# Weight conversion with its clamp moved to GpSimd and its shifted word in PSUM, and three weight tiles placed first

## The chip, the cores and the metric

The kernel runs on one core of one Trainium2 chip. The metric is the device time of one execution in microseconds. Three executions of the kernel before took 1049.48, 1051.94 and 1058.58 us (median 1051.94).

## The reference, cut to what matters

Top-32 attention over 4 batches, 8 heads, 576 tokens and head dimension 64 feeds two dense blocks. Attention keeps, in each row of scores, the 32 largest, and the output is a softmax over those. The first dense block mixes each token with the one before it and computes `sigmoid(xr @ w_r) * (relu(xk @ w_k)^2 @ w_v)`; the second one is `h = gelu(x @ w_in)`, split into u and v, v normalised, mixed over tokens by `w_sg`, multiplied by u, `x + (...) @ w_out`. The weights `w_r, w_k, w_v, w_in, w_out` arrive as float64; the kernel sees them as pairs of 32-bit words and has to turn them into float32 itself, once, before the dense blocks use them.

## The kernel before, in words

**Attention.** Work is cut into 80 row tiles called slots (128 query rows; mostly two heads in one slot). For a slot, `emit_S` (L230) multiplies on TensorE and ScalarE copies the scores to SBUF (L240); `emit_topk` (L255) finds the 32nd largest score on VectorE: an elementwise max and min of the two halves of a row (L272, L273), rounds of MAX8 (L281, L292) and MATCH_REPLACE8 (L287), and at last the masked product with the row sum (L308), after an exponential on ScalarE (L307). `emit_T` (L311) transposes the result through PSUM, and `emit_unit` (L337) multiplies with v and divides by the sums (L372). The q and k rows of a pair of heads are prepared by `prep_pieces` (L158): a copy and a subtraction split each value into two parts (ScalarE L98 or L172, GpSimd L100 or L173), TensorE transposes them, ScalarE copies them out.

**Weight conversion.** `conv` (L380) handles one tile of 128 x 512 weights: 32 tiles of float64 weights, and 5 of `w_sg` that take another branch. For a float64 tile the order is:

- SyncE issues the load of 512 KB of words (L416); H is the high word of each pair, L the low one
- ScalarE takes the absolute value of H, read as a float (L421)
- VectorE clamps it (L422), shifts it by three bits (L423) and joins it with the sign and exponent bits of H (L424)
- ScalarE scales the low word (L425), GpSimd adds it (L426)
- `split` (L96) makes the two parts of the result (ScalarE L98, GpSimd L100), and SyncE stores them to DRAM (L429), from where `wload` (L440) fetches them for every use.

Raw words and intermediate take two of 12 buffers called ring, the result one of 6 called w. The dense blocks (`part1` L478, `part2` L670) take the mixed rows (L489 to L497, the first product is at L502) and the stored weights. Their last adds are at L727, a normalisation at L633.

**Order.** Nothing is ordered by hand but through priorities: `at(p)` (L70) gives what is emitted in it priority p, smaller first. With them a planner (L888) sets, at compile time and by its own model of durations, the order in which each engine's queue holds its instructions. Queues run in that order. Start-up (L774 to L786) has the smallest number and holds the loads and preparation of the first pair of heads, the loads of the second, small constants and the first two slots' scores. Slot s gets 1000*s (L791); up to four conversions are emitted per slot with 1000*(s-4) (L809), dense items with 1000*(s+5)+500 (L816). PSUM has three pools of banks: one for scores, three banks of tag `tp` for transposes and attention output, three of tag `d` for dense products.

Of the kernel before, what the change touches and what calls it, by code (L numbers as in the profile page):

```python
# [11 lines left out]
I32 = mybir.dt.int32  # L12
U32 = mybir.dt.uint32
AF = mybir.ActivationFunctionType
OP = mybir.AluOpType
# [4 lines left out]
CLO = 2.0 ** -15  # L20
CHI = 122879.9921875


def computation(ctx, tc, dram, wscr, flag, fast, q, k, v, mu_k, mu_r, w_k, w_v, w_r, w_in, g_ln, w_sg, b_sg, w_out, out):
    nc = tc.nc
    B, H, S, D = q.shape
# [55 lines left out]
    def bank(tag, shape=(128, 512), dt=F32):  # L82
        if tag == "d" and rows[0] == NROWS:
            tag = ("d", "tp")[turn[0] % 2]
            turn[0] += 1
        return psum.tile(list(shape), dt, tag=tag, name=tag, bufs=BUFS[tag])
# [4 lines left out]
    def ring(shape, name, dt=F32R):  # L91
        return sb.tile(shape, dt, tag="ring", name=name, bufs=NRING)
# [3 lines left out]
    def split(hi, lo, src):  # L96

        nc.scalar.activation(hi, src, AF.Copy)  # L98
        e = nc.vector if tail[0] else nc.gpsimd
        e.tensor_tensor(lo, src, hi.bitcast(F32), op=OP.subtract)  # L100
# [57 lines left out]
    def prep_pieces(su):  # L158

        su.kst, su.qst = {}, {}
        pieces = []
        has1 = 1 in su.chs
        j0, j1 = 2 * su.chs[0], 2 * su.chs[-1] + 2
        nj = j1 - j0
        st = {}

        def spl3(sp, src):  # L170
            n = src.shape[1]
            nc.scalar.activation(sp[:, :n, 0::2, :], src[:, :, None, :].to_broadcast([128, n, 2, D]), AF.Copy)  # L172
            nc.gpsimd.tensor_tensor(sp[:, :n, 1, :], src, sp[:, :n, 0, :].bitcast(F32), op=OP.subtract)  # L173

        def spl_q(h):
            sp = sb.tile([128, 4, 3, D], F32R, tag="splq", name="splq", bufs=1)
            st["q", h] = sp
            spl3(sp, su.raw["q"][:, 4 * h + j0:4 * h + j1, :])

        def spl_k(h):  # L180
            sp = sb.tile([128, 4, 2, D], F32R, tag="splk", name="splk", bufs=1)
            st["k", h] = sp
            split(sp[:, :, 0, :], sp[:, :, 1, :], su.raw["k"][:, 4 * h:4 * h + 4, :])

        def spl_rem():
            sp = sb.tile([128, 2, 3, D], F32R, tag="splr", name="splr", bufs=1)
            st["r"] = sp
            if has1:
                spl3(sp[:, 0:1], su.raw["q"][:, 8:9, :])
            split(sp[:, 1, 0, :], sp[:, 1, 1, :], su.raw["k"][:, 8, :])  # L190

        def main_q(h, c):
            su.qst[h, c] = sb.tile([128, 2, 256], F32R, tag="qst", name="qst", bufs=4)
            ps = bank("tp", (128, 2, 2, 128), F32R)
            j = 2 * (c - su.chs[0])
            for a in range(2):
                for i in range(2):
                    nc.tensor.transpose(ps[:, a, i, :], st["q", h][:, j + i, a:a + 2].rearrange("p a d -> p (a d)"),
                                        identr)
            nc.scalar.activation(su.qst[h, c], ps.rearrange("p a i m -> p a (i m)"), AF.Copy)  # L200

        def main_k(h):
            su.kst[h] = sb.tile([128, S], F32R, tag="kst", name="kst", bufs=4)
            ps = bank("tp", (128, 4, 128), F32R)
            for j in range(4):
                nc.tensor.transpose(ps[:, j, :], st["k", h][:, j].rearrange("p a d -> p (a d)"), identr)
            nc.scalar.activation(su.kst[h][:, 64 * h:64 * h + 512], ps.rearrange("p j m -> p (j m)"), AF.Copy)

        def rem():
            ps = bank("tp", (128, 4, 128), F32R)  # L210
            nc.tensor.transpose(ps[:, 0, :], st["r"][:, 1, 0:2].rearrange("p a d -> p (a d)"), identr)
            for h in range(2):
                nc.scalar.activation(su.kst[h][:, 512 - 512 * h:576 - 512 * h], ps[:, 0, 64 * h:64 * h + 64], AF.Copy)
            if has1:
                for a in range(2):
                    nc.tensor.transpose(ps[:, 1 + a, :], st["r"][:, 0, a:a + 2].rearrange("p a d -> p (a d)"), identr)
                su.qrem = qrems[su.p % 2]
                nc.scalar.activation(su.qrem[:, :, 0::2, :], ps[:, 1:3, :].rearrange("p a (h m) -> p a h m", h=2),
                                     AF.Copy)

        pieces.append(spl_rem)
        for h in range(2):
            pieces.append(lambda h=h: (spl_k(h), main_k(h)))
            pieces.append(lambda h=h: (spl_q(h), main_q(h, su.chs[0])))
            if len(su.chs) == 2:
                pieces.append(lambda h=h: main_q(h, 1))
        pieces.append(rem)
        return pieces
# [151 lines left out]
    def conv(key):  # L380

        kind, i = key
        w = sb.tile([128, 2, 512], F32R, tag="w", name="w", bufs=NW)
        if kind == "sg":
            n = 128 if i < 4 else 64
            raw = ring([128, 5, 128], "rawsg", F32)
            nc.sync.dma_start(raw[:, :4, :n], w_sg[:512, 128 * i:128 * i + n].rearrange("(j p) s -> p j s", p=128))
            nc.sync.dma_start(raw[:64, 4, :n], w_sg[512:, 128 * i:128 * i + n])
            nat = ring([128, S], "nat", F32)
            ps = bank("d", (128, 4, 128))  # L390
            for j in range(4):
                nc.tensor.transpose(ps[:n, j, :], raw[:, j, :n], ident)
            nc.scalar.activation(nat[:n, :512], ps[:n].rearrange("p j m -> p (j m)"), AF.Copy)
            ps = bank("d")
            nc.tensor.transpose(ps[:n, :64], raw[:64, 4, :n], ident[:64, :64])
            nc.scalar.activation(nat[:n, 512:], ps[:n, :64], AF.Copy)
            for hf in range(2):
                if hf:
                    w = sb.tile([128, 2, 512], F32R, tag="w", name="w", bufs=NW)
                split(w[:n, 0, :HALF], w[:n, 1, :HALF], nat[:n, HALF * hf:HALF * hf + HALF])  # L400
                scr = dram.tile([128, 2, HALF], F32, name=f"ws_sg{i}_{hf}")
                nc.sync.dma_start(scr[:n], w[:n, :, :HALF].bitcast(F32))
                wscr["sg", i, hf] = scr
            return
        raw = ring([128, 512, 2], "raw64", I32)
        if kind in ("r", "k", "u"):
            src = {"r": w_r, "k": w_k, "u": w_in}[kind]
            s = src[:, 256 * i:256 * i + 256].rearrange("(c p) f -> p c f", p=128)
        elif kind == "v":
            m, half = divmod(i, 2)  # L410
            s = w_v[512 * half:512 * half + 512, 256 * m:256 * m + 256].rearrange("(c p) f -> p c f", p=128)
        elif kind == "h":
            s = w_in[128 * i:128 * i + 128, 1024:].rearrange("p (c f) -> p c f", f=256)
        else:
            s = w_out[128 * i:128 * i + 128, :].rearrange("p (c f) -> p c f", f=256)
        nc.sync.dma_start(raw.rearrange("p (c f) t -> p c (f t)", c=4), s)  # L416
        H, L = raw[:, :, 1], raw[:, :, 0]
        t2 = ring([128, 2, 512], "cvt", F32)
        a, bb = t2[:, 0], t2[:, 1]
        ai, bi = a.bitcast(I32), bb.bitcast(I32)  # L420
        nc.scalar.activation(a, H.bitcast(F32), AF.Abs)  # L421
        nc.vector.tensor_scalar(a, a, CLO, CHI, op0=OP.max, op1=OP.min)  # L422
        nc.vector.tensor_scalar(ai, ai, 3, 0x3FFFFFFF, op0=OP.logical_shift_left, op1=OP.bitwise_and)  # L423
        nc.vector.scalar_tensor_tensor(bi, H, -0x40000000, ai, op0=OP.bitwise_and, op1=OP.bitwise_or)  # L424
        nc.scalar.activation(ai, L.bitcast(U32), AF.Copy, scale=2.0 ** -29)  # L425
        nc.gpsimd.tensor_tensor(bi, bi, ai, op=OP.add)  # L426
        split(w[:, 0], w[:, 1], bb)
        scr = dram.tile([128, 2, 512], F32, name=f"ws_{kind}{i}")
        nc.sync.dma_start(scr, w.bitcast(F32))  # L429
        wscr[key] = scr  # L430

    convq = deque()
# [332 lines left out]
    for i, t in enumerate(slots):  # L765
        if t.last and t.su.p == NP - 1:
# [3 lines left out]
            elif t.u.ch == 1:  # L770
# [4 lines left out]
    start.__enter__()  # L775
    load_raw(supers[0], [("k", 0, 0), ("q", 0, 0), ("k", 0, 1), ("k", 1, 1), ("k", 1, 0), ("q", 1, 0), ("q", 0, 1),
                         ("q", 1, 1)])
    for pc in prep_pieces(supers[0]):
        pc()
    load_raw(supers[1], "kq")  # L780
# [7 lines left out]
    for s, t in enumerate(slots):  # L788
# [20 lines left out]
        with at(1000 * (s - 4)):  # L809
            for _ in range(min(4, len(convq))):  # L810
                conv(convq.popleft())
# [81 lines left out]
```

## Time and profile before

| what | value |
|---|---|
| runs | 1049.48, 1051.94, 1058.58 us |
| profiled execution | 1051.33 us, of which the span from first to last instruction is 1049.6 us |
| TensorE (PE) busy | 902.5 us, 86% |
| VectorE (DVE) busy | 905.5 us, 86% |
| ScalarE (ACT) busy | 714.9 us, 68% |
| GpSimd (POOL) busy | 490.9 us, 47% |
| granted TensorE clock, mean | 0.906 |

The shares are means over stages that differ. Busy time by stretch, the chain of waits and the groups of one stretch say which engine a stage waits for; a group's mean duration, set beside the shortest instruction in it, says whether its instructions were held up while they ran.

### The profile page before, as it was taken

What the parts mean: (1) busy time and instruction counts of PE and PEld (TensorE: products, weight loads), DVE (VectorE), ACT (ScalarE), POOL (GpSimd) and SP (SyncE); (2) the same over time, 40 slices, a digit from 0 to 9 for tenths busy, and PEclk for the clock granted to TensorE, in tenths of its full rate; (3) what the DMA queues carried; (4) which work ended last, traced back from release to release, by engine and by line L of the source; (5) the groups of instructions that cost most, each with busy time, mean ns of one, the idle gap of its engine ahead of it and who ended that gap; (6) DMA issues with size and microseconds to landing.
All of it is one profiled execution on the core that took longest, in us unless ns stands there. A gap on an engine that the chain in (4) does not pass through costs nothing.

```text
span 1049.6 us, 18933 instructions
## 1 busy us (share of the span) xinstructions
PE 902.5 (86%) x6158; PEld 770.7 (73%) x6158; DVE 905.5 (86%) x2541; ACT 714.9 (68%) x1589; POOL 490.9 (47%) x592
## 2 busy tenths in 40 slices
PE   5144645579989998987899999999999998999997
PEld 4132544468879887855789888878899987799895
DVE  5999999999899999999999999899999989712142
ACT  7666876767898786655778669866786597554340
POOL 3676968823493235660934213679242117310051
PEclk8556656879999998976999999999999999999999
DMA  6676865657755543430334443246333423865432
GB/s 181 202 239 226 253 221 190 203 195 257 262 179 180 181 157 110 146 129 1 95 97 125 121 144 100 67 164 198 110 112 115 133 87 103 300 239 153 115 108 65
DMA packets 103405, 164.36 MB, mean 157 GB/s; under 512 B 19200, under 2 KB 72960, under 8 KB 103296
## 3 DMA queue, kind: packets, MB, share of 16 engines
q1 hardware_dynamic: 103296, 163.05, 48.4%
q8 instruction: 51, 0.84, 0.3%
q14 instruction: 58, 0.48, 0.1%
HBM read 133.09 MB, written 29.92 MB: 155 GB/s over the span
## 4 chain that ended last, share of the span: by engine, by line
PE 40%; DVE 40%; ACT 7%; issue 6%; POOL 4%; DMA 2%; SPq 1%; POOLq 0%; DVEq 0%; ACTq 0%
DVE M L281 9%; DVE T L287 9%; PE d L502 7%; PE d L567 7%; DVE E L308 7%; PE d L691 4%; DVE T L272 3%; PE d L612 3%; PE tp L502 2%; DVE T L273 2%; DVE M L292 2%; PE S L238 2%; PE tp L361 2%; PE tp L321 2%; PE d L719 2%
## 5 line engine op out<-in xcount | busy, mean ns | idle before, releaser
L281 DVE MAX8 M<-T 128x8 f32<-128x288 f32 x576 | 237.7, 444 | 1.7
L287 DVE MATCH_REPLACE8 T<-M,T 128x288 f32<-128x288 f32 x432 | 187.8, 439 | 0.0
L502 PE MATMUL d<-xm,w 128*128 128x288 f32 (+2 forms) x1008 | 159.4, 307 | 5.4 <-ACT xm L98 2.7
L502 PEld LDWEIGHTS d<-xm,w 128*128 128x128 f32 x1008 | 142.9, 195 | 8.7 <-ACT xm L98 3.1
L238 PE MATMUL S<-kst,qst 128*128 128x288 f32 x512 | 115.7, 345 | 36.4 <-ACT S L240 20.6
L308 DVE SCALAR_TENSOR_TENSOR E<-S,kth,E 128x576 f32<-128x576 f32 x144 | 139.4, 1000 | 1.4 <-ACT E L307 0.6
L321 PE MATMUL tp<-ident,E 128*128 128x128 f32 x512 | 85.0, 303 | 53.9 <-DVE E L308 29.8
L238 PEld LDWEIGHTS S<-kst,qst 128*128 128x128 f32 x512 | 85.6, 214 | 46.3 <-ACT S L240 25.2
L321 PEld LDWEIGHTS tp<-ident,E 128*128 128x128 f32 x512 | 66.6, 155 | 59.9 <-ACT cvt L425 23.4
L307 ACT ACTIVATE E<-S,nb 128x576 f32<-128x576 f32 x144 | 105.0, 770 | 1.2
L567 PE MATMUL d<-ksq,w 128*128 128x288 f32 (+2 forms) x672 | 101.9, 300 | 0.0
L240 ACT ACTIVATE S<-S 128x576 f32<-128x576 f32 x128 | 83.6, 653 | 19.3 <-PE S L238 18.2
L567 PEld LDWEIGHTS d<-ksq,w 128*128 128x128 f32 x672 | 91.8, 188 | 0.2
L322 ACT ACTIVATE PT<-tp 128x512 f32<-128x512 f32 x128 | 74.3, 599 | 18.8 <-PE tp L321 18.2
L272 DVE TENSOR_TENSOR T<-S 128x576 f32<-128x576 f32 (+1 forms) x81 | 70.5, 870 | 10.8 <-ACT S L240 10.8
L361 PE MATMUL tp<-PT,rawv 128*64 128x256 f32 (+1 forms) x512 | 77.3, 449 | 0.7 <-ACT PT L322 0.7
L691 PE MATMUL d<-w,vn 128*128 128x288 f32 (+1 forms) x420 | 72.5, 313 | 3.0 <-POOL vn L100 1.1
L100 POOL TENSOR_TENSOR splk<-rawk,splk 128x256 fp32r<-128x256 f32 x40 | 32.4, 811 | 86.0 <-ACT splk L98 73.0
L273 DVE TENSOR_TENSOR T<-S 128x576 f32<-128x576 f32 (+1 forms) x80 | 71.5, 893 | 0.0
L691 PEld LDWEIGHTS d<-w,vn 128*128 128x128 f32 (+1 forms) x420 | 59.2, 190 | 12.6 <-issue 6.7
L100 POOL TENSOR_TENSOR ksq<-tmp,ksq 128x576 fp32r<-128x576 f32 (+2 forms) x32 | 38.2, 1196 | 54.9 <-ACT ksq L98 54.8
L426 POOL TENSOR_TENSOR cvt<-cvt 128x512 int32<-128x512 int32 x32 | 46.8, 1464 | 31.8 <-ACT cvt L425 30.2
(162 smaller groups left out, 2045.6 us busy)
## 6 DMA issues: line engine op xcount, KB each, us to landing
w<-ws_k SPq DMA_DIRECT2D x40, 512.0 KB, 4.1
w<-ws_v SPq DMA_DIRECT2D x40, 512.0 KB, 4.1
w<-ws_r SPq DMA_DIRECT2D x20, 512.0 KB, 6.0
w<-ws_h SPq DMA_DIRECT2D x20, 512.0 KB, 4.0
w<-ws_u SPq DMA_DIRECT2D x20, 512.0 KB, 3.7
w<-ws_sg SPq DMA_DIRECT2D x32, 288.0 KB, 3.2
w<-ws_o SPq DMA_DIRECT2D x16, 512.0 KB, 5.0
rawk<-in_k_dram SPq DMA_DIRECT2D x40, 128.0 KB, 2.3
```

Source lines behind the costliest of these rows:

```text
L238: nc.tensor.matmul(ps[:, hf, :HALF], lhsT=su.qst[h, t.u.ch][:, a, 128 * t.i:128 * t.i + 128], rhs=su.kst[h][:, HALF * hf:HALF * hf + HALF] ...
L272: nc.vector.tensor_tensor(T[:, h, :HALF], t.S[:, h, :HALF], t.S[:, h, HALF:], op=OP.max)
L273: nc.vector.tensor_tensor(T[:, :, HALF:], t.S[:, :, :HALF], t.S[:, :, HALF:], op=OP.min)
L281: nc.vector.max(M[:, h, 8 * r:8 * r + 8], src[h])
L287: nc.vector.match_replace(L[h], M[:, h, 8 * r:8 * r + 8], src[h], NEG)
L307: nc.scalar.activation(E, Sx, AF.Exp, bias=nb[:, h:h + 1], scale=0.125)
L308: nc.vector.scalar_tensor_tensor(E, Sx, kv[h], E, op0=OP.is_ge, op1=OP.mult, accum_out=u.sums[:, c + h:c + h + 1])
L321: nc.tensor.transpose(ps[:, kc, :], E[:, h, 64 * h + 128 * kc:64 * h + 128 * kc + 128], ident)
L361: nc.tensor.matmul(px[64 * h:64 * h + 64, :n], lhsT=vr[:, 4 * h + kc, :], rhs=u.PT[h][:, kc, :n], start=(kc == 0), stop=False)
L502: nc.tensor.matmul(ps[:, :n_], lhsT=w[:, bb, 128 * c:128 * c + 128], rhs=act[ch, which, c][:, a, o:o + n_], start=(c == 0 and i == 0), sto ...
L567: nc.tensor.matmul(ps[:, :nn], lhsT=w[:, bb, 128 * (f % 4):128 * (f % 4) + 128], rhs=kt[f][:, a, o:o + nn], start=(f == 0 and i == 0), sto ...
L691: nc.tensor.matmul(ps[:, :HALF], lhsT=act[b, "vn", i][:nn, a, 128 * m:128 * m + 128], rhs=W["sg", i, si][:nn, bb, :HALF], start=(j == 0), ...
```

## The change

In `conv`, the clamp goes from VectorE to GpSimd (its two operations in the opposite order); the shifted word is written into a new bank of tag `tp` instead of SBUF, and the join reads it there. In start-up, up to three conversions (here three tiles of `w_r`) are emitted between the loads and the preparation of the first pair of heads.

```diff
         nc.scalar.activation(a, H.bitcast(F32), AF.Abs)
-        nc.vector.tensor_scalar(a, a, CLO, CHI, op0=OP.max, op1=OP.min)
-        nc.vector.tensor_scalar(ai, ai, 3, 0x3FFFFFFF, op0=OP.logical_shift_left, op1=OP.bitwise_and)
-        nc.vector.scalar_tensor_tensor(bi, H, -0x40000000, ai, op0=OP.bitwise_and, op1=OP.bitwise_or)
+        nc.gpsimd.tensor_scalar(a, a, CHI, CLO, op0=OP.min, op1=OP.max)
+        pi = bank("tp").bitcast(I32)
+        nc.vector.tensor_scalar(pi, ai, 3, 0x3FFFFFFF, op0=OP.logical_shift_left, op1=OP.bitwise_and)
+        nc.vector.scalar_tensor_tensor(bi, H, -0x40000000, pi, op0=OP.bitwise_and, op1=OP.bitwise_or)
         nc.scalar.activation(ai, L.bitcast(U32), AF.Copy, scale=2.0 ** -29)
...
                          ("q", 1, 1)])
+    for _ in range(min(3, len(convq))):
+        conv(convq.popleft())
     for pc in prep_pieces(supers[0]):
```

## Rows read from the trace of the kernel before

**Rows 1.** Busy time by stretch: us, then each engine's busy us, clock, DMA share, GB/s.
```profile
0.00:26.20 26.20, 13.86 (x62) 11.14 (x62) 14.26 (x43) 18.43 (x41) 10.14 (x25) 0.88 0.65 181
26.20:236.20 210.00, 110.72 (x635) 85.98 (x636) 209.04 (x501) 144.33 (x324) 148.97 (x139) 0.66 0.65 216
236.20:892.20 656.00, 626.94 (x4489) 539.18 (x4489) 628.97 (x1898) 489.38 (x1093) 302.41 (x382) 0.97 0.43 135
892.20:1049.60 157.40, 150.94 (x976) 134.43 (x974) 53.21 (x102) 62.79 (x133) 29.36 (x47) 0.99 0.50 163
472.30:498.60 26.30, 20.70 (x110) 15.26 (x109) 26.03 (x86) 15.54 (x35) 1.53 (x4) 0.68 0.00 1
```

**Rows 2.** The chain of work that ended last, share of the span by engine.
```profile
PE 40%; DVE 40%; ACT 7%; issue 6%; POOL 4%; DMA 2%; SPq 1%; POOLq 0%; DVEq 0%; ACTq 0%
```

**Rows 3.** Groups by line and shape, whole span: count | busy us, mean ns | idle before.
```profile
L100 POOL TENSOR_TENSOR w<-cvt,w 128x512 fp32r<-128x512 f32 x32 | 49.5, 1557 | 4.6 <-ACT w L98 4.6
L426 POOL TENSOR_TENSOR cvt<-cvt 128x512 int32<-128x512 int32 x32 | 46.8, 1464 | 31.8 <-ACT cvt L425 30.2 <-DMA rawv<-in_v_dram 1.3
L424 DVE SCALAR_TENSOR_TENSOR cvt<-raw,cvt 128x512 int32<-128x512 int32 x32 | 32.9, 1028 | 0.0
L422 DVE TENSOR_SCALAR cvt<-cvt 128x512 f32<-128x512 f32 x32 | 24.1, 752 | 1.3 <-ACT cvt L421 1.2
L423 DVE TENSOR_SCALAR cvt<-cvt 128x512 int32<-128x512 int32 x32 | 22.2, 693 | 0.0
```

**Rows 4.** Lines 423, 727 and 633: shortest/median/longest ns, first and last start.
```profile
L423 DVE TENSOR_SCALAR cvt<-cvt x32: 402/498/1500, 21.2 to 226.4; 128x512 int32<-128x512 int32 x32
...
L727 DVE TENSOR_TENSOR xr<-d,xr x12: 668/684/692, 705.9 to 1040.3; 128x512 f32<-128x512 f32 x10, 64x512 f32<-64x512 f32 x2
...
L633 POOL TENSOR_SCALAR tmp<-vraw,bag x20: 763/772/1912, 283.5 to 1009.7; 128x512 f32<-128x512 f32 x16, 64x512 f32<-64x512 f32 x4
```

**Rows 5.** Groups of VectorE, 26.2 to 236.2 us.
```profile
L308 DVE SCALAR_TENSOR_TENSOR E<-S,kth,E 128x576 f32<-128x576 f32 x28 | 27.2, 1005 | 0.2
...
L273 DVE TENSOR_TENSOR T<-S 128x576 f32<-128x576 f32 x12 | 13.6, 1132 | 0.0
...
L372 DVE TENSOR_TENSOR x<-tp,rb 128x256 f32<-128x256 f32 x5 | 2.0, 408 | 0.0
```

**Rows 6.** Groups of VectorE, 472.6 to 498.6 us.
```profile
L308 DVE SCALAR_TENSOR_TENSOR E<-S,kth,E 128x576 f32<-128x576 f32 x7 | 5.4, 802 | 0.0
...
L273 DVE TENSOR_TENSOR T<-S 128x576 f32<-128x576 f32 x2 | 1.5, 750 | 0.0
...
L372 DVE TENSOR_TENSOR x<-tp,rb 128x256 f32<-128x256 f32 x1 | 0.4, 407 | 0.0
```

**Rows 7.** Waits, 26.2 to 236.2 us: us in total, times, longest.
```profile
POOL cvt L426 <- ACT cvt L425: 29.8, 16, 4.1
PE tp L321 <- DVE E L308: 26.5, 8, 7.9
ACT cvt L425 <- DVE cvt L424: 26.1, 19, 3.4
...
ACT w L98 <- POOL cvt L426: 3.6, 7, 1.0
```

**Rows 8.** Start of the timeline: start us, us, engine, line, tile.
```profile
6.79 0.33 SPq L156 DMA_DIRECT2D rawk<-in_k_dram  x1
...
10.70 0.46 DVE L272 TENSOR_TENSOR T<-S 128x288 f32<-128x288 f32 x1 [8.71 <-ACT S L240]
```

**Rows 9.** The chain in order of time, 10 to 30 us: start us, us.
```profile
14.19 5.54 DMA raw<-in_moe_w_r_dram
```

**Rows 10.** Timeline: first row of the third slot; first dense product.
```profile
41.80 1.71 DVE L272 TENSOR_TENSOR T<-S 128x576 f32<-128x576 f32 x1
...
176.61 0.76 PE L502 MATMUL d<-xm,w 128*128 128x256 f32 x2
```

**Rows 11.** Waits of SyncE's queue, whole span.
```profile
SPq L429 <- POOL w L100: 90.0, 29, 13.0
```

## The prediction

> **What bounds the kernel now.** I read the table of busy time by stretch first, because the 86% of VectorE and the 86% of TensorE are means over stages with different limits [rows 1]. From 26.2 to 236.2 us VectorE is busy 209.0 of 210 us, while TensorE is busy 110.7 and GpSimd 149.0: in this stage VectorE sets the pace. All but one or two of the 32 conversions of float64 tiles run in it. From 236.2 to 892.2 us VectorE (629 of 656) and TensorE (627) are both near full, and the last 157 us belong to TensorE alone (151). The chain of waits agrees: 40% on each of the two [rows 2].
>
> Then the groups by line and shape, to see what the conversions take from VectorE: lines 422, 423 and 424 cost 24.1 + 22.2 + 32.9 = 79.2 us [rows 3]. Line 423 needs 402 ns at its shortest, but 693 on the mean, and up to 1500 [rows 3, 4]: most of these instructions are held up while they run. The same holds for the top-32 work with two SBUF inputs: line 308 takes 1005 ns here and 802 in a stretch in which GpSimd is busy 1.5 of 26.3 us; line 273 takes 1132 and 750 [rows 1, 5, 6]. Line 372, which reads one operand from PSUM, takes 408 and 407: it is not stretched [rows 5, 6]. So GpSimd's work costs VectorE time in instructions with SBUF operands alone, and not, as far as a row shows, where an operand lies in PSUM.
>
> **The change, part by part.**
>
> *Clamp off VectorE.* 32 instructions of line 422 go: 24.1 us [rows 3].
>
> *Join reads PSUM.* The nearest row is line 727, 512 elements with one operand in PSUM: 684 ns, never over 692 [rows 4]. I take it: 32 x 0.684 = 21.9 against 32.9 us, 11.0 us less. Bounds: as short as 0.668 (0.5 us better), or unchanged at 1.028, then nothing.
>
> *Shift writes PSUM.* No row shows VectorE writing PSUM. It may keep the shortest time of line 423, 402 ns (9.3 us less than now), or cost what the join costs now, 1028 (10.7 us more). I take the PSUM row of the same length, 684 ns: 22.2 - 21.9 = 0.3 us less. The Trainium skill speaks against this edit (VectorE: DVE Perf Modes, Why PSUM operands drop a tier): an operand in PSUM takes fp32 off the double rate. The trace agrees in so far as no PSUM row of this length is below 668 ns. Priced by line 423's shortest time, the edit would lose 32 x (0.684 - 0.402) = 9.0 us, and the whole sum below would be 13 instead of 22. I go by the 693 that it costs in this stage.
>
> These three make 24.1 + 11.0 + 0.3 = 35.4 us less for VectorE in a stage in which it has no other slack.
>
> *Clamp on GpSimd.* The nearest row is line 633, a two-step scalar instruction on 512 elements: 772 ns median, 763 at least [rows 4]; no row has min or max there. The upper bound is the dearest conversion step there, 1557 [rows 3]: 24.4 to 49.8 us more GpSimd work, and I take 24.7. With it GpSimd is busy 149.0 + 24.7 = 173.7 us in a stage that would last about 180 instead of 210, so its share goes from 0.71 to 0.965. That raises what it costs the top-32 work. The excess now is 28 x 0.203 = 5.7 us on line 308 and 12 x 0.382 = 4.6 on line 273; line 272, as long and as often, I take as another 4.6 [rows 5, 6]. These 14.9 us grow by 0.965/0.71, that is by 5.3 us. (The bound below is zero: the conversion's own VectorE work no longer holds GpSimd up.)
>
> *The new wait.* The shift now waits in VectorE's queue for GpSimd, and all the top-32 work queued behind it waits too. Today one row shows how often GpSimd's conversion step is late for its reader: ScalarE waited for line 426 in 7 of 32 cases, 0.51 us each [rows 7]. With GpSimd near full I take half of the 32: 16 x 0.51 = 8.2 us. Bounds: nothing, and the first rival below.
>
> *A bank of tag tp* is held from the shift's start to the join's end, 1.4 us at least and more when top-32 work runs between. Transposes that need one of the three banks come later. I price it at nothing: in this stage TensorE is idle for 99 of 210 us, and its longest kind of wait is for VectorE anyway (26.5 us on line 308) [rows 1, 7]. If scores came late for that, VectorE would stand still.
>
> *Three tiles first.* For each, a load, a store, three ScalarE, three GpSimd and two VectorE steps and a tp bank move ahead. On SyncE the loads come in front of the second pair's k and q (from 6.79 us), the v and the constants, instead of from 14.19 us [rows 8, 9]. At 5.54 us each, one after the other, they fill 16.6 us from about 4 us on, so the second pair's data land up to that much later; its first VectorE work starts at 41.80 us [rows 10], which covers it. A tile that takes 5.54 us lands at 9.6 us or later, when the first pair's splits are over. So VectorE's 8.71 us of idle time before 10.70 us [rows 8] can hardly be filled, and I take zero. Bounds: 3 x 2 x 0.684 = 4.1 us of gain, or, if the tiles' GpSimd work stood ahead of the first splits, 3 x (0.772 + 1.464 + 1.557) = 11.4 us of loss. The stores wait in SyncE's queue for GpSimd (90.0 us in 29 waits now [rows 11]) with later loads behind them; a chain one step longer adds up to 29 x 0.77 = 22 us of such waits, spread over a stage in which data are fetched a pair ahead. Priced at nothing, with the same proviso as the banks.
>
> **Sum:** 35.4 - 5.3 - 8.2 = 21.9 us. The dense stage starts when the eighth slot's rows are mixed (176.61 us [rows 10]) and slots and dense items keep their order, so what the stage gains should reach the end. The profiled execution took 1051.33 us, 0.6 below the median shown; 1051.9 - 21.9 gives **1030 us**.
>
> **Rivals.**
>
> *GpSimd takes over as the bound (slower).* In the stage it has 61 us of idle time now, 29.8 of it waiting for line 425 [rows 1, 7]. If the 24.7 us came on top of all of this, the stage would last 235 us and the kernel 1077; with 50 of the 61 left, 224 us, and 1066. It decides from the point where more than 210 - 173.7 = 36 us of that idle time can't be used. For it: conversions have smaller priority numbers than the splits of the next pairs, so these stand behind three GpSimd steps per tile, scores come late, and VectorE stands still. Against it: line 425 itself waited 26.1 us for VectorE [rows 7], which becomes quicker, so half of the idle time is of VectorE's making; and conversions can be late without harm until 176 us. The Trainium skill (GPSIMD Engine Reference, Engine selection) gives elementwise work on a tile to VectorE; the trace agrees for a single step, 763 ns at best there against 402 for a like step on VectorE. Chance 0.16.
>
> *The dense stage starts no earlier (no change).* Mixing also runs on GpSimd; if its backlog holds the first dense product at 177 us, TensorE, 96% busy from 236 us on [rows 1], ends when it did: 1042 to 1052 us. The planner's new order could do the same. For it: the full TensorE. Against it: the backlog would have to outlast 22 us. Chance 0.17.
>
> *PSUM does not do what it should (no change).* If the join stays at 1028 and the shift costs 1028 too, the sum is 24.1 - 10.7 - 13.5 = 0; if only the join stays, 10.9 us are left: 1041 to 1052. Chance 0.07.
>
> **How the numbers follow.** The forecast has 0.60. Its own range goes from 35.4 + 9.3 + 4.1 = 49 us of gain (1003) to 1041. The range that I give leaves out a tenth at either end: 1008 on one side, and on the other 1060, the milder half of the first rival. About 1% (10.5 us) is what a measurement of this kernel tells from no change. Faster by more: 0.60 and a little of the milder ends of the second and third rival, 0.63. Within it: 0.21. Slower: the first rival, 0.16.
>
> **What would show it.** In the changed profile lines 423 and 424 should each take about 684 ns with little spread, the clamp about 0.8 us on GpSimd, and lines 308 and 272 to 273 slightly more than now. VectorE's waits for the clamp should stay below 10 us, and the first dense product should come at about 155 us. Wrong would be: VectorE idle for tens of microseconds behind the clamp or behind ScalarE's copies of scores; a dense start that doesn't move; a shift of 1 us.

## The result, and the profile after

The change made the kernel slower. After it the median of 4 executions is 1066.53 us, beside 1051.51 us for the kernel before on the same chip: a ratio of 1.0134 [1.0092, 1.0176]. The forecast was 1030, its range 1008 to 1060. The profiled execution took 1067.13 us with a span of 1065.4, 15.8 us more than before. In A and F below one execution each was slow (1555.96 and 2839.48 us); their medians and ratios are of the others.

The page's busy times and the chain of waits, as [rows 2] for before:

```profile
PE 905.1 (85%) x6158; PEld 766.8 (72%) x6158; DVE 887.0 (83%) x2509; ACT 712.0 (67%) x1587; POOL 504.1 (47%) x624
...
DVE 43%; PE 30%; ACT 10%; issue 5%; DMA 5%; POOL 4%; SPq 1%; POOLq 0%; DVEq 0%; ACTq 0%
```

VectorE lost 18.5 us of work (905.5 before), yet the span grew. Busy time by stretch shows where (columns as in [rows 1]; the last row is longer than before's by the 15.8 us of the span):

```profile
0.00:26.20 26.20, 3.40 (x18) 2.67 (x18) 4.81 (x11) 11.95 (x23) 13.87 (x28) 1.00 0.72 211
26.20:236.20 210.00, 118.92 (x638) 91.19 (x639) 180.53 (x464) 145.91 (x332) 152.18 (x170) 0.71 0.63 213
236.20:892.20 656.00, 617.88 (x4436) 526.28 (x4436) 632.93 (x1886) 482.61 (x1085) 302.26 (x374) 0.98 0.41 131
892.20:1065.40 173.20, 164.90 (x1069) 146.64 (x1069) 68.77 (x149) 71.53 (x151) 35.76 (x54) 0.99 0.50 162
```

In the stage that VectorE bounded, it now stands still for 29.5 of 210 us (before: 1.0), and in the first 26.2 us it works 4.8 (before: 14.3). GpSimd has hardly more to do in the stage, 152.2 against 149.0. So the stage has lost its bound, and no engine has taken VectorE's place.

The conversion's own groups, whole span, as [rows 3], and then the shortest, median and longest of three lines, as [rows 4] (from line 424 on, a line of before has become the next one: the join is now 425, GpSimd's addition 427):

```profile
L100 POOL TENSOR_TENSOR w<-cvt,w 128x512 fp32r<-128x512 f32 x32 | 43.9, 1373 | 5.7 <-ACT w L98 5.7
L427 POOL TENSOR_TENSOR cvt<-cvt 128x512 int32<-128x512 int32 x32 | 43.7, 1369 | 26.3 <-DVE cvt L425 10.6 <-ACT cvt L426 10.2 <-DVE kth L296 4.7
L422 POOL TENSOR_SCALAR cvt<-cvt 128x512 f32<-128x512 f32 x32 | 22.4, 701 | 17.2 <-ACT cvt L421 16.8
L424 DVE TENSOR_SCALAR tp<-cvt 128x512 int32<-128x512 int32 x32 | 21.7, 681 | 17.6 <-POOL cvt L422 11.4 <-ACT PT L322 6.0
L425 DVE SCALAR_TENSOR_TENSOR cvt<-raw,tp 128x512 int32<-128x512 int32 x32 | 21.4, 673 | 0.1
```

```profile
L422 POOL TENSOR_SCALAR cvt<-cvt x32: 602/612/1122, 9.1 to 205.7; 128x512 f32<-128x512 f32 x32
...
L424 DVE TENSOR_SCALAR tp<-cvt x32: 666/680/696, 9.8 to 211.6; 128x512 int32<-128x512 int32 x32
...
L425 DVE SCALAR_TENSOR_TENSOR cvt<-raw,tp x32: 657/673/689, 12.1 to 212.6; 128x512 int32<-128x512 int32 x32
```

No duration is above its forecast: VectorE's share of a conversion went from 79.2 to 43.1 us in all, and shift and join have lost their spread. What is new stands behind the second bar of the line-424 row: VectorE waits there for the clamp and, 6.0 us, for a ScalarE copy of transposes (line 322), which has nothing to do with conversions but the PSUM tag. The waits of the stage, as [rows 7], show the same link in the other direction:

```profile
ACT cvt L426 <- DVE tp L424: 16.7, 12, 4.4
...
DVE E L308 <- ACT E L307: 14.2, 2, 12.5
...
DVE T L272 <- ACT S L240: 12.0, 2, 9.2
...
PE tp L321 <- DVE E L308: 10.4, 3, 8.2
...
PE tp L206 <- DVE cvt L425: 9.8, 2, 8.4
```

Transposes of k (line 206) wait for the *join* of a conversion, and VectorE itself waits for scores and exponentials (lines 240 and 307). Two stretches of the timeline show how one leads to the other. The first is the start, as [rows 8]:

```profile
3.46 0.72 POOL L100 TENSOR_TENSOR splk<-rawk,splk 128x256 fp32r<-128x256 f32 x1 [1.95 <-ACT splk L98]
...
9.77 0.69 DVE L424 TENSOR_SCALAR tp<-cvt 128x512 int32<-128x512 int32 x1 [7.78 <-POOL cvt L422]
...
12.12 0.69 DVE L425 SCALAR_TENSOR_TENSOR cvt<-raw,tp 128x512 int32<-128x512 int32 x1
...
12.96 0.72 PE L206 MATMUL tp<-identr,splk 128*128 128x128 f32 x4 [12.96 <-POOL cvt L422]
...
13.70 0.69 DVE L425 SCALAR_TENSOR_TENSOR cvt<-raw,tp 128x512 int32<-128x512 int32 x1
14.53 0.72 PE L198 MATMUL tp<-identr,splq 128*128 128x128 f32 x4 [0.85 <-DVE cvt L425]
16.41 0.66 ACT L421 ACTIVATE cvt<-raw 128x512 f32<-128x512 f32 x1 [3.62 <-DMA raw<-in_moe_w_r_dram]
...
19.25 0.58 ACT L207 ACTIVATE kst<-tp 128x512 fp32r<-128x512 f32 x1
...
28.44 0.46 DVE L272 TENSOR_TENSOR T<-S 128x288 f32<-128x288 f32 x1 [9.22 <-ACT S L240]
```

The split k is ready at 4.18 us, and TensorE does nothing until 12.96. The three tiles placed first take the three tp banks, so the first transposes get the bank of the first word, which is free when the first join ends (12.12 + 0.69 = 12.81); the next transposes follow the second join's end (14.39) at 14.53. The row names a clamp as the releaser of the first wait; it ends at 12.93 us, but the transposes don't read it. In the trace TensorE's wait for VectorE's semaphore ends at 12.85, just behind the join. The first top-32 work starts at 28.44 us, against 10.70 [rows 8]. Of these 17.7 us the bank's wait is 8.7. Another 5.6 lie in ScalarE's queue: its copy of the first transposes (line 207), which end at 13.68, starts at 19.25, behind conversion steps of which one waits 3.62 us for its load.

The second is the longest gap of VectorE in the stage (timeline, three engines):

```profile
202.86 0.60 PE L321 MATMUL tp<-ident,E 128*128 128x128 f32 x4
...
208.79 0.67 DVE L424 TENSOR_SCALAR tp<-cvt 128x512 int32<-128x512 int32 x1
...
210.20 0.68 DVE L425 SCALAR_TENSOR_TENSOR cvt<-raw,tp 128x512 int32<-128x512 int32 x1
...
210.93 1.12 PE L321 MATMUL tp<-ident,E 128*128 128x128 f32 x4 [7.47 <-DVE cvt L425]
...
213.35 0.47 PE L324 MATMUL tp<-ident,E 128*128 128x128 f32 x1 [1.30 <-DVE cvt L425]
...
221.88 0.55 PE L206 MATMUL tp<-identr,splk 128*128 128x128 f32 x4
...
231.52 0.65 PE L238 MATMUL S<-kst,qst 128*128 128x288 f32 x3
...
234.35 0.82 ACT L307 ACTIVATE E<-S,nb 128x576 f32<-128x576 f32 x1
235.20 0.82 DVE L308 SCALAR_TENSOR_TENSOR E<-S,kth,E 128x576 f32<-128x576 f32 x1 [12.54 <-ACT E L307]
```

From 203.46 to 210.93 TensorE waits for a bank whose turn belongs to a word that VectorE doesn't write before 208.79: the shift stands in VectorE's queue behind top-32 work. The word itself holds its bank for 2.1 us. Everything in TensorE's queue behind these transposes, the next pair's transposes and scores among them, comes later by that, and from 222.66 us on VectorE has nothing left to select. Not all of the 12.54 us is this wait's: the chain of waits between the two also has a load of q, 3.53 us from 226.40.

**The balance, by marks.** There are 144 instructions of line 308, one or two at the end of each slot's top-32 work. The start of the nth is a mark that doesn't depend on where the clock reads 26.2 or 236.2. (The expectations below call the 41st mark that of the 21st slot; by the count of line 308 in each slot it is the 23rd's.) From before to after, the 1st moves from 25.7 to 40.5 us (14.8 later). From the 1st to the 17th after is 16.5 us quicker (130.0 for 146.5): there the saving is. From the 17th to the 41st it is 16.2 us longer (160.5 for 144.3), with VectorE idle for 25.6 us (before 6.7). From the 41st to the end it is 1.3 longer. That makes the 15.8 us. All traces, by the same marks (us; each from one profiled execution, and the total of one kernel differs by 2 to 10 us between executions, so a difference of a few us between two marks decides nothing):

| kernel | 1st | 17th | 41st | 143rd | span | VectorE idle, 17th to 41st |
|---|---|---|---|---|---|---|
| before | 25.7 | 172.2 | 316.5 | 886.3 | 1049.6 | 6.7 |
| after | 40.5 | 170.5 | 331.0 | 903.7 | 1065.4 | 25.6 |
| A conversion alone | 22.9 | 149.6 | 341.5 | 908.8 | 1068.6 | 50.1 |
| B tiles first alone | 30.1 | 185.2 | 330.8 | 907.1 | 1064.3 | 17.1 |
| C after, word in tag d | 29.2 | 140.9 | 296.0 | 868.5 | 1041.3 | 11.9 |
| D conversion alone, word in d | 23.6 | 144.9 | 292.6 | 864.3 | 1035.4 | 3.8 |
| E as D, fewer conversions ahead | 23.7 | 145.1 | 294.0 | 865.1 | 1035.0 | 2.0 |
| F clamp alone | 23.7 | 155.6 | 303.6 | 876.1 | 1046.8 | 4.9 |
| G PSUM alone, word in d | 25.7 | 162.9 | 307.6 | 888.2 | 1049.1 | 8.0 |
| H before, constants earlier | 25.6 | 174.8 | 318.4 | 892.3 | 1063.9 | 5.8 |
| I after, tiles behind preparation | 30.2 | 161.0 | 321.7 | 894.1 | 1057.6 | 24.6 |
| J as D, constants earlier | 24.1 | 145.6 | 290.7 | 865.5 | 1033.2 | 2.3 |
| K after, constants earlier | 39.8 | 171.3 | 334.2 | 903.1 | 1063.6 | 27.4 |
| L as A, four tp, two d | 22.9 | 144.8 | 329.9 | 906.0 | 1084.2 | 40.8 |
| M before, two tp, four d | 24.6 | 172.0 | 321.8 | 947.9 | 1093.4 | 11.9 |
| N as D, word in a tag of its own | 23.4 | 151.6 | 299.4 | 876.0 | 1058.8 | 7.3 |

### The profile page after: what moved, and what is told of

Read it like the earlier page. It is cut to its first block, busy times and chain, and to the rows that moved or that the text cites. A ratio compares the mean times of both kernels' runs of the same rounds, so it can differ in the third digit from the quotient of the medians.

```text
span 1065.4 us, 18973 instructions
## 1 busy us (share of the span) xinstructions
PE 905.1 (85%) x6158; PEld 766.8 (72%) x6158; DVE 887.0 (83%) x2509; ACT 712.0 (67%) x1587; POOL 504.1 (47%) x624
## 4 chain that ended last, share of the span: by engine, by line
DVE 43%; PE 30%; ACT 10%; issue 5%; DMA 5%; POOL 4%; SPq 1%; POOLq 0%; DVEq 0%; ACTq 0%
DVE M L281 11%; DVE T L287 10%; DVE E L308 7%; PE d L568 5%; PE d L503 4%; DVE T L272 4%; DVE T L273 4%; PE d L692 3%; DVE M L292 3%; PE tp L361 3%; PE d L613 3%; PE tp L503 2%; PE S L238 1%; ACT E L307 1%; PE d L720 1%
## 5 line engine op out<-in xcount | busy, mean ns | idle before, releaser
L281 DVE MAX8 M<-T 128x8 f32<-128x288 f32 x576 | 238.2, 444 | 1.6
L308 DVE SCALAR_TENSOR_TENSOR E<-S,kth,E 128x576 f32<-128x576 f32 x144 | 147.1, 1052 | 19.6 <-ACT E L307 19.1
L503 PE MATMUL d<-xm,w 128*128 128x288 f32 (+2 forms) x1008 | 155.8, 303 | 6.6 <-POOL xm L100 3.8
L503 PEld LDWEIGHTS d<-xm,w 128*128 128x128 f32 x1008 | 139.9, 191 | 10.2 <-POOL xm L100 5.1
L321 PE MATMUL tp<-ident,E 128*128 128x128 f32 x512 | 86.3, 306 | 36.6 <-DVE E L308 16.2
L240 ACT ACTIVATE S<-S 128x576 f32<-128x576 f32 x128 | 83.6, 653 | 23.9 <-PE S L238 20.8
L273 DVE TENSOR_TENSOR T<-S 128x576 f32<-128x576 f32 (+1 forms) x80 | 80.6, 1007 | 0.0
L272 DVE TENSOR_TENSOR T<-S 128x576 f32<-128x576 f32 (+1 forms) x81 | 68.8, 849 | 14.0 <-ACT S L240 13.9
L100 POOL TENSOR_TENSOR splk<-rawk,splk 128x256 fp32r<-128x256 f32 x40 | 34.7, 866 | 68.6 <-ACT splk L98 51.7
L292 DVE MAX8 M<-T 128x8 f32<-128x288 f32 x144 | 58.4, 441 | 0.0
```

The lines of the kernel that those rows point to most:

```text
L272: nc.vector.tensor_tensor(T[:, h, :HALF], t.S[:, h, :HALF], t.S[:, h, HALF:], op=OP.max)
L273: nc.vector.tensor_tensor(T[:, :, HALF:], t.S[:, :, :HALF], t.S[:, :, HALF:], op=OP.min)
L281: nc.vector.max(M[:, h, 8 * r:8 * r + 8], src[h])
L308: nc.vector.scalar_tensor_tensor(E, Sx, kv[h], E, op0=OP.is_ge, op1=OP.mult, accum_out=u.sums[:, c + h:c + h + 1])
L321: nc.tensor.transpose(ps[:, kc, :], E[:, h, 64 * h + 128 * kc:64 * h + 128 * kc + 128], ident)
L503: nc.tensor.matmul(ps[:, :n_], lhsT=w[:, bb, 128 * c:128 * c + 128], rhs=act[ch, which, c][:, a, o:o + n_], start=(c == 0 and i == 0), sto ...
```

## The experiments

The theory was that the word's place in tag tp costs the gain; the rivals were the clamp on GpSimd, the three tiles, and the number of banks.

**A. The conversion as changed, without the three tiles.**

```diff
-    for _ in range(min(3, len(convq))):
-        conv(convq.popleft())
```

> The conversion as changed (clamp on GpSimd, shifted word in a tp bank), without the three tiles first. Theory (tp banks: a transpose waits until the join on VectorE frees its bank): VectorE's first top-32 work back at about 11 us, but TensorE still waits for the join in the stage to 240 us and VectorE still has idle gaps of 10 to 25 us there; 1040 to 1055 us. Rival (GpSimd's backlog sets the stage): GpSimd's waits and the late scores stay and cost what they cost; 1060 us or more.

1070.33 us, 1.0186 [1.0165, 1.0206]. The theory's number missed, and the time lies in the rival's range; C and D decide between the two. Without the tiles the start is fine (1st mark 22.9), but the stage is worse than in the whole change (41st mark 341.5), so the cause is in the conversion. The waits of the stage, and the timeline around one gap:

```profile
PEld tp L321 <- DVE cvt L425: 23.4, 4, 9.9
...
PE tp L321 <- DVE cvt L425: 22.2, 4, 9.5
```

```profile
106.09 0.58 ACT L322 ACTIVATE PT<-tp 128x512 f32<-128x512 f32 x1
...
106.77 1.33 DVE L424 TENSOR_SCALAR tp<-cvt 128x512 int32<-128x512 int32 x2 [6.81 <-ACT PT L322]
```

TensorE waited for joins for 22.2 us. And the tag binds VectorE too: at 106.77 the shift had waited 6.81 us for ScalarE to empty a bank of transposes, with all top-32 work behind it.

**B. The three tiles first, with the conversion of before.**

```diff
+    for _ in range(min(3, len(convq))):
+        conv(convq.popleft())
     for pc in prep_pieces(supers[0]):
```

> The three tiles first, with the conversion of the kernel before (no PSUM bank in it). Theory (tp banks): the first transposes don't wait for a conversion, VectorE's first top-32 work comes at 10.7 to 14 us, 1045 to 1057 us. Rival (the three tiles' loads and steps themselves hold up the first pair): first top-32 work at 18 us or later, 1060 to 1070 us.

1067.46 us, 1.0164 [1.0136, 1.0192]; the theory expected less, and the time lies in the rival's range. But the first transposes come at 4.20 us here and the first top-32 work at 11.67, where the rival wanted 18 or later, so nothing is held at the start, and the 1st mark is 4.4 us later than before's, not 14.8. The other 10 us to the 41st mark stay unexplained; with the conversion of D the same edit costs 3.4 there (C).

**C. The whole change, with the word in a bank of tag d.**

```diff
-        pi = bank("tp").bitcast(I32)
+        pi = bank("d").bitcast(I32)
```

> The whole change, with the shifted word in a bank of tag d (dense products) instead of tp. Theory (tp banks): first top-32 work at 11 to 15 us, no waits of transposes for the join, VectorE busy over 97% from 26 to 210 us; 1022 to 1040 us. Rival (GpSimd sets the stage): VectorE still idle for 20 us or more there; over 1052 us.

1044.14 us, 0.9942 [0.9922, 0.9963], 4 us above the theory's range and 8 below the rival's. One word of the program is changed, though the planner orders the queues anew for it (J and K bear on that), and the 41st mark is 35.0 us earlier than in after. The start (timeline) and the stage (busy time by stretch):

```profile
4.27 0.75 PE L206 MATMUL tp<-identr,splk 128*128 128x128 f32 x4 [4.27 <-POOL splk L100]
...
9.79 0.69 DVE L424 TENSOR_SCALAR d<-cvt 128x512 int32<-128x512 int32 x1 [7.80 <-POOL cvt L422]
...
12.00 0.46 DVE L272 TENSOR_TENSOR T<-S 128x288 f32<-128x288 f32 x1 [0.79 <-ACT S L240]
```

```profile
26.20:236.20 210.00, 123.93 (x752) 97.96 (x754) 202.89 (x551) 156.88 (x367) 161.29 (x176) 0.72 0.68 224
```

The first word is at 9.79 us as in after, but the transposes don't wait for it, and top-32 work starts at 12.00 instead of 28.44. In the stage VectorE is busy for 202.9 instead of 180.5 us while GpSimd does more than in after (161.3 against 152.2). Both the clamp's place and the tiles' place are as in after, so neither by itself is what cost the time.

**D. The conversion alone, with the word in d** (A and C together).

> The conversion as changed but with the shifted word in a bank of tag d, and no tiles first. Theory (tp banks): 1024 to 1040 us, within 6 us of the kernel with both parts and a d bank. Rival (GpSimd sets the stage): over 1052 us, and no better than the same with a tp bank.

1037.74 us, 0.9877 [0.9858, 0.9896]: faster than both kernels, 32.6 us below A. Its groups of VectorE in the stage:

```profile
L308 DVE SCALAR_TENSOR_TENSOR E<-S,kth,E 128x576 f32<-128x576 f32 x29 | 29.9, 1061 | 0.3
...
L273 DVE TENSOR_TENSOR T<-S 128x576 f32<-128x576 f32 x13 | 15.0, 1156 | 0.0
...
L424 DVE TENSOR_SCALAR d<-cvt 128x512 int32<-128x512 int32 x30 | 20.4, 679 | 0.1
```

The shift's wait for the clamp has shrunk to 0.1 us in 30 instructions. The 41st mark is 23.9 us earlier than before's.

**E. As D, but fewer conversions ahead of the first dense product** (one per slot in slots 6 and 7).

```diff
-            for _ in range(min(4, len(convq))):
+            for _ in range(min((4 if s < 6 or s > 7 else 1), len(convq))):
```

> Clamp on GpSimd, shifted word in a d bank, no tiles first, and six conversions fewer emitted ahead of the first dense block (one each in slots 6 and 7 instead of four). Theory (the first dense product waits for weight loads that stand in SyncE's queue behind stores of later conversions): first dense product at 150 to 170 us instead of 185, total 1020 to 1034 us. Rival (the dense start is held by GpSimd's mixing or by TensorE): no earlier than 180 us, total 1034 to 1042 us, as with four in each slot.

1036.07 us, 0.9851 [0.9821, 0.9881]. This tests whether the start of the dense stage sets the end. First, D (waits of SyncE's queue, 120 to 190 us; first dense product), then E (first dense product):

```profile
SPq L430 <- POOL w L100: 21.2, 6, 6.6
```

```profile
184.68 2.50 PE L503 MATMUL d<-xm,w 128*128 128x256 f32 x10 [3.75 <-DMA w<-ws_r]
```

```profile
160.77 2.86 PE L503 MATMUL d<-xm,w 128*128 128x256 f32 x12
```

In D the weights' loads stand in SyncE's queue behind stores that wait for GpSimd, and the first product comes at 184.7 us. In E it comes 24 us earlier, as the theory had it, yet the span is only 0.4 us shorter, and the total is in the rival's range. Here the dense stage's start doesn't set the end.

**F and G. Clamp alone; PSUM alone (in d).** F is the kernel before with the first line of this diff changed, G is D with that line changed back:

```diff
-        nc.vector.tensor_scalar(a, a, CLO, CHI, op0=OP.max, op1=OP.min)
+        nc.gpsimd.tensor_scalar(a, a, CHI, CLO, op0=OP.min, op1=OP.max)
```

> The kernel before with the clamp alone moved to GpSimd; shift and join stay in SBUF. Theory (the clamp's 24 us on VectorE are worth most, and GpSimd has room): 1034 to 1046 us, with lines 423 and 424 still stretched to 0.6 to 1.1 us. Rival (the PSUM operand pays, the clamp only moves the load into instructions that GpSimd holds up): 1046 to 1056 us.

> The kernel before with the shifted word alone in a d bank; the clamp stays on VectorE. Theory (the join falls from 1.03 to 0.69 us and the shift stays at 0.69): 11 us less for VectorE, 1038 to 1046 us. Rival (the clamp is what pays): 1046 to 1054 us.

F: 1051.71 us, 1.0002 [0.9983, 1.0020]. G: 1047.10 us, 0.9954 [0.9931, 0.9978]. By their totals both lie in the rivals' ranges. At the 41st mark F is 12.9 us ahead of before and G 8.9: together 21.8, and D has 23.9. In its median F has lost all of it by the end.

**H. The kernel before, with the small constants loaded ahead of the first v** (no work added or removed; only the planner's order changes).

```diff
-    load_raw(supers[0], "v")
     load_const()
+    load_raw(supers[0], "v")
```

> The kernel before, with the small constants loaded ahead of the first pair's v instead of behind it: the same work, but the planner comes to another order in all queues. Theory (a new order alone is worth little): 1046 to 1056 us, first top-32 work at about 11 us. Rival (the order alone moves the kernel by more than 1%): below 1041 or above 1061 us.

1068.38 us, 1.0162 [1.0141, 1.0183], where 1046 to 1056 was expected. An edit without any work costs as much as the change studied. But it does so elsewhere: the 41st mark is 1.9 us late, the 143rd 6.0, the end 14.3; from the 143rd mark on it takes 171.6 instead of 163.3 us.

**I. After, with the three tiles emitted behind the preparation.**

> The changed kernel with the three tiles emitted behind the first pair's preparation instead of ahead of it; the word stays in a tp bank. Theory (banks of a tag go round in the order in which they are asked for in the program, so that the first transposes stand behind three conversions): first top-32 work at 10.5 to 14 us instead of 28.4, the gaps of the later stage remain, 1050 to 1068 us. Rival (the tiles' loads and GpSimd steps hold up the first pair): first top-32 work at 20 us or later.

1058.59 us, 1.0072 [1.0052, 1.0092]. The first top-32 work is at 11.90 us, and 9.3 us are won at the 41st mark: the start's part is the turn that the tiles take ahead of the first transposes. The gap of the stage is still there (timeline):

```profile
225.31 0.82 DVE L308 SCALAR_TENSOR_TENSOR E<-S,kth,E 128x576 f32<-128x576 f32 x1 [12.35 <-ACT E L307]
```

**J and K. D and after, each with the edit of H.**

> Clamp on GpSimd, word in a d bank, no tiles first, and the small constants loaded ahead of the first pair's v (the edit that alone made the kernel before 16 us slower). Theory (the stage's gain of some 24 us is of the conversion, the order moves what comes after): 21st slot's masked product at 288 to 298 us, total 1025 to 1052 us. Rival (the gain was luck of the order): 21st slot after 305 us, total over 1052 us.

> The changed kernel with the small constants loaded ahead of the first pair's v. Theory (the tp bank costs the stage 35 us or more against a d bank, in whatever order): 21st slot at 322 to 345 us, total 1055 to 1080 us. Rival (the loss is an accident of one order): 21st slot before 310 us, total under 1053 us.

J: 1039.37 us, 0.9898 [0.9878, 0.9918]; K: 1065.07 us, 1.0133 [1.0097, 1.0168]. The 41st marks move by -1.9 and +3.2 us, and all four values lie in the ranges of the theory, so the verdict on the two places of the word doesn't hang on one order.

**L. As A, with four tp banks and two of d.**

```diff
-    BUFS = {"S": 1, "tp": 3, "d": 3}
+    BUFS = {"S": 1, "tp": 4, "d": 2}
```

> The conversion as changed (word in a tp bank), no tiles first, with four tp banks and two d banks instead of three and three. Theory (three tp banks are too few for transposes and words together): VectorE idle under 12 us between 90 and 240 us, 21st slot at 295 to 320 us; with a d bank less the dense part may be slower, total 1035 to 1062 us. Rival (it is not the number of banks but that a transpose stands behind a join at all): VectorE idle over 25 us there, 21st slot after 330 us.

1085.65 us, 1.0328 [1.0305, 1.0351]. If tp only had a bank too few, a fourth would have cured the stage. It gives back 11.6 of the 48.9 us that A loses to D at the 41st mark, and VectorE still idles for 40.8. The missing d bank may hide some of the cure: N, which lacks it too, is 6.8 us behind D at that mark.

**M. The kernel before, with two tp banks and four of d.**

> The kernel before (no word in PSUM) with two tp banks and four d banks. If tp banks are scarce in the stage, as the tp bank's holding by a conversion would need, VectorE is idle for 15 us or more between 26 and 240 us and the 21st slot comes after 328 us. If two banks do for the transposes and it is the standing behind a join that costs, VectorE idle stays under 8 us there and the 21st slot comes at 310 to 324 us.

1095.43 us, 1.0420 [1.0378, 1.0461]. Transposes that have only two banks, but share them with nothing, lose 5.3 us at the 41st mark, and VectorE stands idle for 2.3 us between 26 and 240 us. The large loss comes later (41st to 143rd: 626.1 for 569.8 us); no run asked why, and it has no part in this question.

**N. As D, with the word in a bank of its own tag, and two of d.**

```diff
-    BUFS = {"S": 1, "tp": 3, "d": 3}
+    BUFS = {"S": 1, "tp": 3, "d": 2, "cv": 1}
...
-        pi = bank("d").bitcast(I32)
+        pi = bank("cv").bitcast(I32)
```

> Clamp on GpSimd, no tiles first, the word in a bank with a tag of its own (one bank), tp left at three, d reduced to two. If the cost lies in sharing the tag's turns with the transposes, the stage is as good as with a d bank: 21st slot at 288 to 302 us, VectorE idle under 18 us from 26 to 270 us (the dense part, short of a d bank, may then be slower: total 1035 to 1062 us). If the cost lies in the word being in PSUM and the wait for GpSimd, or one bank for the words is too few, the 21st slot comes after 315 us.

1055.62 us, 1.0045 [1.0024, 1.0067]. A single bank for words keeps most of the gain at the 41st mark (17.1 us ahead of before, VectorE idle 7.3); but from the 143rd mark to the end it takes 182.8 us, in D 171.0. The missing d bank may be the reason (L, the other kernel with two, takes 178.3 there); no run shows it by itself.

## Why the prediction was wrong

The step that failed: **"A bank of tag `tp` ... I price it at nothing".** It measured 48.9 us at the 41st mark without the tiles (A against D) and 35.0 with them (after against C); at the end 32.6 and 22.4 us. The argument was that TensorE is idle for 99 of 210 us, so that late transposes would be made up. But that idle time was no reserve: as the two timelines of after read, TensorE's work here is a chain with VectorE's and ScalarE's (transposes, copies, scores, selection), and a late link moves all that is queued behind it. The prediction wrote "If scores came late for that, VectorE would stand still", and gave that no price. It is what happened: 44.2 of A's 48.9 us lie between the 17th and the 41st mark, and there VectorE is idle for 50.1 us, in D for 3.8. L and M show that the count of banks is at most a smaller part of the cause, and N, which gives back 42.1 of the 48.9 us, that a bank apart from the transposes is a cure. That the two take turns in the program's order, whichever is ready, is read from the two timelines of after, and I agrees at the start; no run changed that rule by itself.

The steps in turn:

- *VectorE bounds the stage*: right. Where nothing shares the tag, less VectorE work makes the stage shorter (D, F, G).
- *Clamp off, join and shift at 0.684 us*: right: at the median 0.673 and 0.680 us; 79.2 - 43.1 = 36.1 us less against 35.4. The Trainium skill (VectorE: DVE Perf Modes, Why PSUM operands drop a tier) takes the double rate from fp32 with a PSUM operand; the trace agrees, for int32 words: no shift is below 666 ns, where line 423 took 402 at best. What the mean of 693 had cost I read as waiting for GpSimd, and it went: line 424 never takes over 696. The Trainium skill (SBUF — State Buffer, SBUF: two separate sides) lets a VectorE instruction contend with GpSimd when it runs in a two-port mode or has two SBUF inputs; the trace agrees for the join, with one (at most 689 ns, while line 308, with two, takes 1061 on the mean in D's stage).
- *Clamp on GpSimd at 0.772 us*: 0.701 on the mean, 22.4 us for 24.7. *Excess on top-32 work, +5.3*: about right in after, 6.1 in the stage (26 x 0.099 on line 308, 12 x 0.217 on line 273, 11 x 0.082 on line 272); in D none is left (lines 308 and 273 take 56 and 24 ns more on the mean, line 272 157 less). *The wait for the clamp, 8.2*: 0.1 in D; in after 11.4, of which 7.78 at the start, when VectorE had nothing else.
- *The sum, 21.9 us*: with the word in d the 41st mark gains 23.9; clamp and PSUM alone gain 12.9 and 8.9, where the terms gave 24.1 - 5.3 - 8.2 = 10.6 and 11.3. (The range's far end, 49 us of gain, counts 0.3 us of the shift twice; nothing hangs on it.)
- *Three tiles first at zero*: at the start wrong by the failed step again, 17.6 us at the 1st mark (after against A). By the 41st mark the tiles have turned into a gain of 10.5 us, and at the end they leave 3.8: without them the loss would have been larger. No run shows why. With the word in d they cost 5.6 us at the 1st mark, 3.4 at the 41st and 6.4 at the end (C against D). That the first pair's data are not held up by the tiles' loads was right (transposes at 4.27 us in C). *The stores* don't wait longer on SyncE's queue: 36.9 us in 16 waits, where 90.0 in 29 stood [rows 11].
- *What the stage gains should reach the end*: half wrong. Of D's 23.9 us, 14.2 are left in the span: 1.9 go between the 41st and the 143rd mark, 7.7 after it. An edit with no work in it loses 8.3 us in that last part (H against before), so I take this for the planner's order of the last stage and not a cost of the conversion; that is an inference from H, J and F, whose last parts take 167.7 to 171.6 us, and not shown. The dense start, forecast at 155 us, came at 195.0 in after, and it is not what carries a gain to the end (E).
- *GpSimd as the bound* gave 1066 for its milder half, which is the time that came, by another mechanism: GpSimd is at 152.2 us in the stage, not 174, and C has more of its work in a kernel 22 us faster. One of the signs of being wrong that the prediction named did come, by the failed step: in the stage VectorE waits 12.0 us behind ScalarE's copies of scores and 14.2 behind its exponentials. *The dense stage starts no earlier*: in D it starts 8 us later than before, in a faster kernel. *PSUM does not do what it should*: no; it was the tag, not the memory.

## What to carry to other kernels

A buffer taken from a pool that other engines' work rotates through is a wait in both directions, and its price is not the time for which it is held but the place of the holder's instructions in their queues. Before borrowing one, ask whose chain the pool serves: here the banks of dense products, of which the first came at 177 us, let the whole forecast gain of the stage through (23.9 us at the 41st mark in D), and those of the transposes cost up to 49 us more. And where a planner orders the queues, run one edit without any work in it: here that moved the total by 1.6%, so that only marks inside the stage could tell the parts apart.

## What had not been expected of the hardware

GpSimd's clamp of 128 x 512 floats took 612 ns at the median in after and 615 in D, where the nearest row, a two-step scalar instruction of the same size, took 772; in F, where VectorE's shift and join still have all operands in SBUF, it took 777 (605 at least). VectorE writing int32 words to PSUM from SBUF took 680 ns, as long as reading them from there (673), with a spread of 30 ns, next to 376 to 1477 ns for the same shift into SBUF in F.
